# A chunk's final state made in four column groups and brought to its rows by four VectorE instructions

## The chip, the cores and the metric

The kernel runs on one core of a Trainium2 chip, in one launch. The metric is device microseconds of one execution. The engines are named as in the profile: PE (TensorE, matrix products), PEld (its weight loads), DVE (VectorE), ACT (ScalarE), POOL (GpSimd), SP (the queue that issues most DMAs). Three executions of the kernel before took 619.65, 619.74 and 620.53 us; the median is 619.74 us.

## What is computed

The first stage is a state-space scan over 4 batches, 8 heads, 768 tokens, with 32 values of `x` and 16 states for each head. Its output, 3072 rows of 256, goes through two feed-forward layers (256 to 2048 to 256, the first with an ELU, the second with Mish), all in fp32.

```python
for c in range(nc):                      # chunks of tokens
    cum = np.cumsum(la, axis=-1)         # la = log of the clipped decay a
    L = np.exp(cum[:, :, :, None] - cum[:, :, None, :]) * causal
    M = np.einsum('bhin,bhjn->bhij', Cc, Bc) * L
    y_intra = np.einsum('bhij,bhjd->bhid', M, xc)
    y_inter = np.einsum('bhin,bhnd->bhid', Cc, state) * decay_to_i[:, :, :, None]
    y[:, :, sl] = y_intra + y_inter
    Bx = np.einsum('bhjn,bhjd->bhjnd', Bc, xc) * decay_from_j[:, :, :, None, None]
    state = decay_full[:, :, None, None] * state + np.sum(Bx, axis=2)
```

The result doesn't depend on the length of a chunk; the reference uses 32 tokens, the kernel 96.

## The kernel before

**The scan.** A tile `i` is one chunk of 96 tokens of one batch; there are 8 chunks of 4 batches, 32 tiles, and tile `i + 4` is the next chunk of the same batch (`NB` is 4, `T` is 96). Its input `x_t[i]` has 128 rows: rows 0 to 95 are the tokens, 256 columns for the 8 heads; rows 96 to 127 hold the state that came out of the chunk before. A state row belongs to one of the two heads of a pair (16 states each) and has 64 columns for each of the four pairs, in which only the 32 columns of its own head may be other than zero. `rr_t[i]`, as tall, holds the decayed scores of the tokens and, below, the decayed C. So one product over 128 rows (`at_y`, L707) gives a head's within-chunk and from-state parts together. The eight heads' products are 32 rows by 96 columns each; head `h` writes the rows `32 * (h % 4)` on of the PSUM tile `ys`.

**The state.** `at_st` (L737) makes the four pairs' products of `bw_t[i]`, which holds the decayed B of the tokens and, from the second chunk on, the decay of the old state on a diagonal, with `x_t[i]`: 32 rows by 64 columns for a pair. All four are written to rows 96 to 127 of `ys`, side by side in columns 256 to 511. `at_st_out` (L746) is one DVE instruction over 32 rows and 256 columns: it multiplies by the mask `pm`, which keeps each head's own half, and writes rows 96 to 127 of `x_t[i + 4]`. In the last chunk (the last four tiles) no state is made, so there are 28 such tiles. In the first chunk `at_st` of the four tiles stands apart from `at_y`, and the four share one PSUM tile, so each one's products wait for the copy of the one before. From the second chunk on `at_y` and `at_st` are one step on PE, one behind the other, in one buffer of the two of the ring `s`. That buffer is given back when the state's copy and both parts of y (`at_y_hi` on ACT, L719, `at_y_lo` on DVE, L724) have been read; the scores of the next tile (`at_scores0`, L658, in the early tiles; `at_scores`, L670, later) use the same ring, and DVE multiplies them by the decays (L664, L676) before the next `at_y`.

**The feed-forward layers.** They run in blocks of 384, 512 or 256 tokens. A slot is 128 of the 2048 inner columns of a block: `emit_h` (L779 to L781) makes them as three products of split fp32r numbers, ACT and DVE apply the nonlinearity (L795 to L811, L826) and split the outcome (L366, L368, L822), and `emit_y1` (L842 to L847) or `emit_y2` (L873, L874) adds them to the output. The 32 pairs of weight tiles are split on ACT, DVE and POOL as they come in (L340 to L382).

**The order.** No order of instructions is written out: each piece of work is a `step` with an engine (some may choose between two), a planned duration and the steps that it needs; `run_steps` deals them to the engines one after another by these durations and by how late each may begin, and each engine then runs its list in that order. So a step's planned duration doesn't change the work, but it can change the order on every engine. The steps of this change are those at L1099, L1100, L1154 and L1155.

Of the kernel before, what the change touches and what calls it, by code (L numbers as in the profile page):

```python
# [13 lines left out]
ALU = mybir.AluOpType  # L14
# [4 lines left out]
def tile_chain(  # L19
# [12 lines left out]
    nc = tc.nc  # L32
    NB, H, S, D = x.shape
    N = Bm.shape[-1]
    T = 96
# [33 lines left out]
    A, V, G, PE, DQ = "act", "dve", "pool", "pe", "sp"  # L69
# [13 lines left out]
    def step(opts, *deps, dl=1e9):  # L83
        steps.append((opts if isinstance(opts, list) else [opts], deps, dl))
        return len(steps) - 1
# [20 lines left out]
    class Need:  # L106
# [10 lines left out]
        d=Ring(2), r=Ring(1), t=Ring(1), r1=Ring(1), bw=Ring(2), o=Ring(2), stk=Ring(1),  # L117
# [142 lines left out]
    c_t, b_t, c96_t, x_t = {}, {}, {}, {}  # L260
# [468 lines left out]
    def at_st(i):  # L729
        if i == 0:  # L730
            new_ys(i)
        elif i < NB:
            ys_t[i] = ys_t[0]
        kr = 128 if i >= NB else T
        bw, xs = bw_t.pop(i), x_t[i]
        for q in range(H // 2):
            nc.tensor.matmul(  # L737
                out=ys_t[i][T:128, 256 + 64 * q:256 + 64 * q + 64],
                lhsT=bw[0:kr, q, :],
                rhs=xs[0:kr, q * 64:(q + 1) * 64],  # L740
                start=True,
                stop=True,
            )

    def at_st_out(i):
        nc.vector.tensor_tensor(  # L746
            out=x_t[i + NB][T:128].rearrange("p (q e) -> p q e", e=64),
            in0=ys_t[i][T:128, 256:512].rearrange("p (q e) -> p q e", e=64),
            in1=pm[T:128].rearrange("p g d -> p (g d)").unsqueeze(1).to_broadcast([32, H // 2, 64]),
            op=ALU.mult,  # L750
        )


    st = {}
# [199 lines left out]
    for j, (key, k) in enumerate(jobs):  # L954
        rn, pn = [], []
# [141 lines left out]
    for i in range(NB):  # L1097
        bf, bw = BW[i]
        sp_ = step((PE, 0.19, lambda i=i: at_st(i)), bw, LX[i], an, SO.get(i - 1, []))  # L1099
        SO[i] = step((V, 0.41, lambda i=i: at_st_out(i)), sp_, LX[i + NB])  # L1100
        bf.append(sp_)
        xf[i].append(sp_)
    af.append(SO[NB - 1])

    for i in range(NB, tiles):
        c, b = divmod(i, NB)
        bcf, bcn = take("bc")
        lb = step((DQ, 0.96, lambda i=i: load_bc(i), 1.9), bcn)
        l96 = step((DQ, 1.44, lambda i=i: load_c96(i), 0.15), lb)
        d_f, d_n = take("d")  # L1110
        lc = step((DQ, 0.48, lambda i=i: at_cumrow(i), 0.82), s_q4[c], d_n)
        cold = i in TR0
        if cold:
            pf, pn = take("s")
            tr = step((PE, 0.6, lambda i=i: at_tr0(i)), lb, pn)
            tf, tn = take("t")
            a2 = step(alt(lambda e, i=i: at_tr0_out(i, e), (A, 0.37), (V, 0.47)), tr, tn)
            pf.append(a2)
        else:
            a2, a5, tf = three_parts(i, lb)  # L1120
        dd = []
        for g in range(2):
            f = lambda e, i=i, g=g: at_diff(i, g * H // 2, (g + 1) * H // 2, e)
            dd.append(step(alt(f, (G, 1.0), (V, 0.47)), lc, s_q6))
            lock.add(dd[-1])
        mk = step((G, 0.95, lambda i=i: at_mask(i)), dd)
        ex = step((A, 0.78, lambda i=i: at_exp(i)), mk)
        table[ex] = "exp"
        cs = step((G, 0.95, lambda i=i: at_cs(i)), l96, lc, s_d5)
        r_f, r_n = take("r")  # L1130
        rc = step((V, 0.56, lambda i=i: at_rc(i)), cs, r_n)
        rc2 = step(alt(lambda e, i=i: at_rc2(i, e), (V, 0.37), (A, 0.52)), rc)
        lock.add(rc2)
        bcf += [a2, cs]
        if c + 1 < NCH:
            bf, bn = take("bw")
            b1 = step((G, 0.42, lambda i=i: at_bw_1(i)), lb, s_d3, bn)
            b2 = step((G, 0.42, lambda i=i: at_bw_2(i)), s_d7, b1)
            bcf.append(b1)
        if cold:  # L1140
            pz = []
            for z in range(2):
                two = [take("s"), take("s")]
                sc = step((PE, 0.65, lambda i=i, z=z: at_scores0(i, z)), a2, [n for _, n in two])
                tf.append(sc)
                pz.append(step((V, 0.61, lambda i=i, z=z: at_p0(i, z)), sc, ex, r_n))
                for pf, _ in two:
                    pf.append(pz[-1])
        else:
            pz = two_scores(i, a5, tf, ex, r_n, False)  # L1150
        d_f += pz + [rc]
        pf, pn = take("s")
        if c + 1 < NCH:
            y = step((PE, 0.76, lambda i=i: (at_y(i), at_st(i))), pz, rc, rc2, LX[i], pn, SO[i - NB], b1, b2)  # L1154
            SO[i] = step((V, 0.41, lambda i=i: at_st_out(i)), y, LX[i + NB])  # L1155
            pf.append(SO[i])
            bf.append(y)
        else:
            y = step((PE, 0.57, lambda i=i: at_y(i)), pz, rc, rc2, LX[i], pn, SO[i - NB])
        r_f.append(y)  # L1160
        pf += out_of_y(i, y)
        xf[i].append(y)
# [111 lines left out]
```

## Time and profile before

| what | before |
|---|---|
| median of three executions | 619.74 us |
| span of the profiled execution | 618.0 us |
| PE busy | 605.9 us, 98% |
| DVE busy | 433.2 us, 70% |
| ACT busy | 384.6 us, 62% |
| POOL busy | 179.1 us, 29% |
| products of the state, L737 | 224 instructions in 28 tiles |
| copies of the state, L746 | 28 instructions, 430 ns each |

The profile is of one execution whose span, from its first instruction to its last, is 618.0 us, 1.7 us under the median. A line of the profile names the source line, the engine, the operation and what is written from what; `x8` is a number of instructions. A product of fp32 numbers counts as two instructions on PE. Products are pipelined, so the duration of one is longer than the time by which it delays the next; what the chain of waits gives to a group is the time in which it held the path. "Idle before" is how long the engine stood still before an instruction, with what released it.

### The profile page before, as it was taken

How to read it: one execution, taken by the hardware profiler on the slowest of the kernel's cores; microseconds unless marked ns; L12 is line 12 of the kernel's file. 1: busy time of each engine (PE TensorE's matmuls, PEld its weight loads, DVE VectorE, ACT ScalarE, POOL GpSimd, SP SyncE). 2: the span in 40 equal slices, each digit the busy share in tenths (PEclk: the TensorE clock that was granted, in tenths of full speed). 3: DMA queues.
4: the chain of work that ended last, by engine and by line, in shares of the span. 5: the costliest groups of instructions: out<-in, count | busy, mean ns of one | idle time of the engine just before them, and what ended most of it. 6: DMA issues, size and time to landing. Idle time of an engine off the chain costs nothing.

```text
span 618.0 us, 10932 instructions
## 1 busy us (share of the span) xinstructions
PE 605.9 (98%) x3876; PEld 515.0 (83%) x3876; DVE 433.2 (70%) x877; ACT 384.6 (62%) x712; POOL 179.1 (29%) x222
## 2 busy tenths in 40 slices
PE   6999999999999999999999999999999999999997
PEld 5777799899988878888888888888888888988896
DVE  4889899987787788655877865777765445744454
ACT  4699999988788876444596643687544314642121
POOL 2366445332555564011445400236100000200000
PEclk9599999999999999999999999999999999999999
DMA  7699982305467553002474301543300000100010
GB/s 156 175 266 301 295 210 77 60 7 100 104 98 106 104 98 59 2 0 46 77 110 72 82 1 14 108 75 87 60 0 1 1 2 9 27 2 0 1 36 18
DMA packets 133655, 47.09 MB, mean 76 GB/s; under 512 B 116672, under 2 KB 122432, under 8 KB 133600
## 3 DMA queue, kind: packets, MB, share of 16 engines
q1 hardware_dynamic: 133488, 46.29, 34.2%
q8 instruction: 30, 0.49, 0.3%
q14 instruction: 25, 0.20, 0.1%
q10 hardware_dynamic: 112, 0.10, 0.0%
HBM read 32.31 MB, written 3.24 MB: 58 GB/s over the span
## 4 chain that ended last, share of the span: by engine, by line
PE 97%; DMA 1%; DVE 1%; issue 0%; ACT 0%
PE h L779 15%; PE acc L873 15%; PE h L781 14%; PE h L780 14%; PE acc L874 7%; PE acc L842 6%; PE acc L844 6%; PE acc L843 6%; PE acc L847 3%; PE ys L707 3%; PE ys L737 2%; PE s L670 1%; PE s L658 1%; DMA t<-stk 1%; PE p_tr L620 1%; PE p_cr L637 0%
## 5 line engine op out<-in xcount | busy, mean ns | idle before, releaser
L779 PE MATMUL h<-xyh,wi 128*128 128x512 f32 (+2 forms) x448 | 166.9, 373 | 0.0
L780 PE MATMUL h<-xyl,wi 128*128 128x512 f32 (+2 forms) x448 | 161.9, 361 | 0.0
L781 PE MATMUL h<-xyh,wi 128*128 128x512 f32 (+2 forms) x448 | 161.7, 361 | 0.0
L873 PE MATMUL acc<-wo,gh 128*128 128x512 f32 x384 | 142.7, 403 | 0.0
L822 DVE TENSOR_TENSOR gl<-w,gh 128x512 fp32r<-128x512 f32 (+2 forms) x182 | 121.2, 668 | 26.2 <-ACT gh L366 17.2
L826 ACT ACTIVATE w<-h 128x512 f32<-128x512 f32 (+2 forms) x112 | 58.9, 536 | 100.7 <-PE h L781 66.3
L874 PE MATMUL acc<-wo,gl 128*128 128x256 f32 x384 | 107.6, 280 | 0.0
L779 PEld LDWEIGHTS h<-xyh,wi 128*128 128x128 f32 x448 | 84.8, 189 | 14.9 <-DVE g L809 0.2
L368 DVE CAST gh<-w 128x512 fp32r<-128x512 f32 (+2 forms) x110 | 45.3, 412 | 73.8 <-PE acc L873 47.6
L781 PEld LDWEIGHTS h<-xyh,wi 128*128 128x128 f32 x448 | 84.9, 190 | 10.8
L780 PEld LDWEIGHTS h<-xyl,wi 128*128 128x128 f32 x448 | 85.0, 190 | 8.7
L873 PEld LDWEIGHTS acc<-wo,gh 128*128 128x128 f32 x384 | 72.2, 188 | 15.7
L795 ACT ACTIVATE w<-h 128x512 f32<-128x512 f32 (+2 forms) x96 | 51.7, 540 | 47.4 <-PE h L781 33.7
L366 ACT ACTIVATE gh<-w 128x512 fp32r<-128x512 f32 (+2 forms) x98 | 57.4, 586 | 29.3 <-PE acc L843 24.2
L874 PEld LDWEIGHTS acc<-wo,gl 128*128 128x128 f32 x384 | 72.5, 189 | 2.0
L822 POOL TENSOR_TENSOR gl<-w,gh 128x512 fp32r<-128x512 f32 (+2 forms) x26 | 29.7, 1141 | 153.1 <-ACT gh L366 120.2
L842 PE MATMUL acc<-gh,wo 128*128 128x512 f32 (+2 forms) x192 | 70.1, 365 | 0.0
L843 PE MATMUL acc<-gh,wo 128*128 128x512 f32 (+2 forms) x192 | 69.6, 363 | 0.0
L844 PE MATMUL acc<-gl,wo 128*128 128x512 f32 (+2 forms) x192 | 69.6, 362 | 0.0
L803 DVE TENSOR_SCALAR w<-w 128x512 f32<-128x512 f32 (+2 forms) x69 | 28.7, 415 | 26.1 <-ACT w L795 25.2
L811 DVE TENSOR_TENSOR w<-h,w 128x512 f32<-128x512 f32 (+2 forms) x69 | 43.4, 628 | 1.7
L844 PEld LDWEIGHTS acc<-gl,wo 128*128 128x128 f32 x192 | 36.2, 188 | 5.1
(103 smaller groups left out, 847.0 us busy)
## 6 DMA issues: line engine op xcount, KB each, us to landing
d<-cum_d SPq DMA_DIRECT2D x31, 288.0 KB, 3.9
raw<-in_moe_w_in_dram SPq DMA_DIRECT2D x16, 512.0 KB, 6.0
raw<-in_moe_w_out_dram SPq DMA_DIRECT2D x16, 512.0 KB, 6.1
xs<-in_x_dram SPq DMA_DIRECT2D x32, 96.0 KB, 2.9
bc<-in_C_dram SPq DMA_DIRECT2D x32, 48.0 KB, 3.1
bc<-in_B_dram SPq DMA_DIRECT2D x32, 48.0 KB, 3.0
out_dram<-o SPq DMA_DIRECT2D x15, 96.0 KB, 1.9
bc<-bc SPq DMA_DIRECT2D x84, 16.0 KB, 2.3
```

The lines of the kernel that those rows point to most:

```text
L366: nc.scalar.activation(out=out, in_=in_, func=AF.Copy)
L779: nc.tensor.matmul(out=h, lhsT=hi[:, k, fs], rhs=xh[:, k, :], start=(k == 0), stop=False)
L780: nc.tensor.matmul(out=h, lhsT=hi[:, k, fs], rhs=xl[:, k, :], start=False, stop=False)
L781: nc.tensor.matmul(out=h, lhsT=lo[:, k, fs], rhs=xh[:, k, :], start=False, stop=(k == 1))
L795: nc.scalar.activation(out=new_w(s), in_=st[s][0], func=AF.Exp)
L822: alu(eng).tensor_tensor(out=gl, in0=w, in1=gh.bitcast(F32), op=ALU.subtract)
L826: nc.scalar.activation(out=new_w(s), in_=st[s][0], func=AF.Mish)
L842: nc.tensor.matmul(out=y, lhsT=hi[:, f % FP, ds], rhs=gh, start=(f == 0), stop=False)
L843: nc.tensor.matmul(out=y, lhsT=lo[:, f % FP, ds], rhs=gh, start=False, stop=False)
L844: nc.tensor.matmul(out=y, lhsT=hi[:, f % FP, ds], rhs=gl, start=False, stop=(f == NF - 1))
L873: nc.tensor.matmul(out=y, lhsT=gh[:, ts], rhs=w[:, :, f % FP, :], start=(f == 0), stop=False)
L874: nc.tensor.matmul(out=y[:, 0], lhsT=gl[:, ts], rhs=w[:, 0, f % FP, :], start=False, stop=(f == NF - 1))
```

## The change

Pair `q` of the state is written to rows `32 * q` to `32 * q + 31` of `ys`, in columns 256 to 319, so each of the four products has a column group of its own. As the four pairs no longer stand on one set of rows, the copy into rows 96 to 127 of the next chunk's tile becomes four DVE instructions of 32 rows and 64 columns, each from another set of rows. The planned durations follow: the copy's from 0.41 to 0.95 us, that of `at_y` with `at_st` from 0.76 to 0.65 us.

```diff
     def at_st(i):
...
         for q in range(H // 2):
             nc.tensor.matmul(
-                out=ys_t[i][T:128, 256 + 64 * q:256 + 64 * q + 64],
+                out=ys_t[i][32 * q:32 * q + 32, 256:320],
                 lhsT=bw[0:kr, q, :],
                 rhs=xs[0:kr, q * 64:(q + 1) * 64],
...
     def at_st_out(i):
-        nc.vector.tensor_tensor(
-            out=x_t[i + NB][T:128].rearrange("p (q e) -> p q e", e=64),
-            in0=ys_t[i][T:128, 256:512].rearrange("p (q e) -> p q e", e=64),
-            in1=pm[T:128].rearrange("p g d -> p (g d)").unsqueeze(1).to_broadcast([32, H // 2, 64]),
-            op=ALU.mult,
-        )
+        for q in range(H // 2):
+            nc.vector.tensor_tensor(
+                out=x_t[i + NB][T:128, 64 * q:64 * q + 64],
+                in0=ys_t[i][32 * q:32 * q + 32, 256:320],
+                in1=pm[T:128].rearrange("p g d -> p (g d)"),
+                op=ALU.mult,
+            )
...
-        SO[i] = step((V, 0.41, lambda i=i: at_st_out(i)), sp_, LX[i + NB])
+        SO[i] = step((V, 0.95, lambda i=i: at_st_out(i)), sp_, LX[i + NB])
...
-            y = step((PE, 0.76, lambda i=i: (at_y(i), at_st(i))), pz, rc, rc2, LX[i], pn, SO[i - NB], b1, b2)
-            SO[i] = step((V, 0.41, lambda i=i: at_st_out(i)), y, LX[i + NB])
+            y = step((PE, 0.65, lambda i=i: (at_y(i), at_st(i))), pz, rc, rc2, LX[i], pn, SO[i - NB], b1, b2)
+            SO[i] = step((V, 0.95, lambda i=i: at_st_out(i)), y, LX[i + NB])
```

## Rows read from the trace of the kernel before

**Rows 1.** The page: busy us, share of the span and instructions of each engine.

```profile
PE 605.9 (98%) x3876; PEld 515.0 (83%) x3876; DVE 433.2 (70%) x877; ACT 384.6 (62%) x712; POOL 179.1 (29%) x222
```

**Rows 2.** Waits of PE: line and what it waited for, us in total, times, longest.

```profile
PE p_cr L637 <- DVE cum L439: 4.4, 1, 4.4
...
PE s L658 <- DVE r L664: 0.9, 1, 0.9
...
PE ys L707 <- DVE r L676: 0.4, 1, 0.4
PE p_d L493 <- ACT dk L366: 0.2, 1, 0.2
```

**Rows 3.** The chain that ended last, whole span: shares by line.

```profile
by line: PE h L779 15.1%; PE acc L873 14.9%; PE h L781 14.3%; PE h L780 14.3%; PE acc L874 7.2%; PE acc L842 6.3%; PE acc L844 6.2%; PE acc L843 6.2%; PE acc L847 3.3%; PE ys L707 2.6%; PE ys L737 2.1%; PE s L670 1.5%; PE s L658 1.5%; DMA t
```

**Rows 4.** The chain from 154 to 161 us: start, us, what.

```profile
155.43 0.47 PE ys L707 x16
155.90 0.45 PE ys L737 x8
156.34 0.38 PE h L779
...
159.67 0.36 PE s L670 x8
```

**Rows 5.** L707 in short stretches: stretch, length, busy us (instructions in flight) of PE.

```profile
155.34:155.40 0.06, 0.04 (x4) 0.04 (x7) 1.00 1.09 307
...
155.62:155.66 0.04, 0.04 (x16) 0.04 (x4) 1.00 0.16 39
```

**Rows 6.** The same view of L737, two of its first stretches.

```profile
155.72:155.78 0.06, 0.05 (x1) 0.06 (x2) 1.00 0.37 111
...
155.89:155.95 0.06, 0.06 (x4) 0.06 (x3) 1.00 0.95 248
```

**Rows 7.** The same view of L658, four products on two row groups.

```profile
64.01:64.10 0.09, 0.08 (x2) 0.08 (x2) 1.00 0.54 147
...
64.18:64.20 0.02, 0.02 (x4) 0.02 (x5) 1.00 1.63 419
```

**Rows 8.** The chain from 22 to 37 us: the first chunk's state products.

```profile
23.57 0.99 PE ys L737 x8
...
35.18 0.90 PE ys L737 x16
```

**Rows 9.** L746 by stretch: stretch, length, busy us (instructions) of DVE.

```profile
0.00:137.00 137.00, 3.87 (x9) 0.95 0.65 175
```

**Rows 10.** All engines by stretch: PE, PEld, DVE, ACT, POOL busy us, granted clock.

```profile
24.00:137.00 113.00, 112.50 (x730) 97.21 (x728) 102.87 (x203) 105.69 (x201) 55.92 (x58) 0.98 0.63 173
137.00:420.00 283.00, 282.33 (x1836) 236.26 (x1835) 206.47 (x405) 190.08 (x338) 100.81 (x129) 1.00 0.39 71
```

**Rows 11.** Groups on DVE by shape: out and in, number, busy us, mean ns, idle before.

```profile
L746 DVE TENSOR_TENSOR xs<-ys,pm 32x256 f32<-32x256 f32 x28 | 12.1, 430 | 11.3 <-ACT xyh L719 5.9 <-PE ys L737 4.9
L724 DVE SCALAR_TENSOR_TENSOR xyl<-ys,xyh 128x192 fp32r<-128x192 f32 x29 | 10.3, 354 | 1.4 <-ACT xyh L719 1.0
L724 DVE SCALAR_TENSOR_TENSOR xyl<-ys,xyh 128x64 fp32r<-128x64 f32 x3 | 0.7, 221 | 1.0 <-ACT xyh L719 1.0
```

**Rows 12.** DVE in order of time: start, us, instruction.

```profile
22.08 0.68 DVE L382 TENSOR_TENSOR wi<-raw,wi 128x512 fp32r<-128x512 f32 x1
22.68 0.35 DVE L724 SCALAR_TENSOR_TENSOR xyl<-ys,xyh 128x192 fp32r<-128x192 f32 x1
...
33.95 0.43 DVE L746 TENSOR_TENSOR xs<-ys,pm 32x256 f32<-32x256 f32 x1
34.41 0.70 DVE L358 SCALAR_TENSOR_TENSOR raw<-raw 128x512 int32<-128x512 int32 x1
...
157.35 0.36 DVE L724 SCALAR_TENSOR_TENSOR xyl<-ys,xyh 128x192 fp32r<-128x192 f32 x1
```

**Rows 13.** The stretch of the low granted clock: engines as in rows 10.

```profile
15.25:28.90 13.65, 12.66 (x127) 10.32 (x124) 11.71 (x31) 8.72 (x19) 3.94 (x4) 0.50 0.61 162
```

## The prediction

> **What bounds the kernel now.** I read the page's busy shares and slices first [rows 1]. PE is busy in 605.9 of 618.0 us; DVE has 70% and ACT 62%. The span is 1.7 us short of the median of the runs shown (619.74); what lies around the span I take as constant, so a gain in the span is a gain in the median. Then PE's waits: six in all, from 4.4 us to 0.2, together 7.6 us, of which the 4.4 us is the start; the other five make 3.2 us [rows 2]. So for nearly the whole span nothing else makes PE wait, and a microsecond of PE work taken away is a microsecond off the span, until another engine becomes late. The chain that ended last says the same: PE's lines fill it, and L737, the line that the change touches, has 2.1% of it, 13.0 us [rows 3]. Last I read engines by stretch [rows 10], because DVE and ACT don't have the same room everywhere. Until 137 us the weights are prepared and PE, ACT and DVE are all near full (112.5, 105.7 and 102.9 of 113 us from 24 us on); from 137 to 420 us PE is full and DVE has 206.5 of 283.
>
> **The removed PE time.** In an ordinary tile the chain holds the 16 instructions of L707 (eight heads, two instructions each) for 0.47 us and then the 8 of L737 (four pairs, two each) for 0.45 us [rows 4]. Twice the instructions, half as wide again, in the same time: the counts of instructions in flight show why. L707's enter four at a time: 4 are begun in the first 0.06 us and 16 after 0.3 [rows 5]. Its heads go to column groups 0, 1, 2, 3 in turn. L737's enter one at a time, 1 in the first 0.06 us and 4 after 0.2 [rows 6]; all four pairs go to column group 3, so each waits for the one in front. The change gives pair q column group q. It should then go as L707 does, in two rounds of four. That this also holds for four products only, both instructions of each, is seen at L658: four products on two row groups enter in pairs, 2 and then 4 [rows 7]. It isn't the same arrangement, but it shows that the second instruction of a product doesn't stand between its neighbours' first ones.
>
> A round should take what one instruction takes now, 0.45 / 8 = 0.056 us; two rounds 0.11 us, and 0.34 us is saved in a tile. The bounds for two rounds: 0.11 us, and two of L707's rounds at full width, 2 x 0.47 / 4 = 0.24 us, which holds also the change from the wide product in front. I take 0.11, because L737 mostly follows L707 directly, and the change to the next wide product (0.38 us, [rows 4]) is paid now as then. The first tile ran at half the granted clock [rows 13]: 0.99 us [rows 8], and six instructions fewer of twice 0.056 us save 0.67 there. Sum: 0.67 + 27 x 0.34 = 9.9 us of the 13.0. Of the 28 tiles [rows 11] 9 lie before 137 us [rows 9] and 19 behind: 0.67 + 8 x 0.34 = 3.4 us early, 19 x 0.34 = 6.5 us late.
>
> **The added DVE time.** One instruction of 32x256 took 430 ns. What four of 32x64 take no row shows. Above, each could cost the whole 430; below, a quarter of it, and then nothing is added (less is excluded, since the same elements are read). L724 reads the same tile at several widths: 354 ns at 192 and 221 at 64 [rows 11], which is 1.04 ns an element, and L746's 430 at 256 lies on the same line. So I take 0.22 us each. Do they overlap? Many neighbours on DVE do: an instruction of 0.68 us from 22.08 was followed at 22.68. After L746 it isn't so: 0.43 us from 33.95, the next at 34.41 [rows 12]. I take the second kind, 0.25 us from start to start, so 1.0 us for four against 0.46 now: 0.54 us more in each tile, 15 us in all. The Trainium skill gives this a rule ("VectorE: DVE Perf Modes", section "Two Vector instructions with no wait between them"): an instruction that starts in another quadrant (a set of 32 rows) of a memory than the one before it is held until all earlier ones are done. The gap after L746, which writes rows 96 to 127, agrees; the four new ones each read another quadrant, so by the rule they would not overlap either.
>
> Where the 0.54 us lie: behind 137 us DVE has 76 us of idle time for 19 x 0.54 = 10.3, and nothing on PE waits for L746 directly, as its rows are read four tiles later. The PSUM buffer of a tile is held 0.54 us longer: in the tile above L724, the last to read it, ended at 157.71 [rows 12], and the next scores came at 159.67 [rows 4], so 1.4 of 2.0 us remain. In the first four tiles, which share one buffer, the next product waits for the copy: the copy from 33.95 ended at 34.38 and the chain reached the next L737 at 35.18 [rows 8, 12], so some 0.3 of 0.8 us remain. I cost both at nothing; without that cover each tile would pay up to 0.54. Behind the four instructions on DVE stand the lower half of the split of y (L724), the products of scores and decays (L676) and the FFN's elementwise steps, and PE waits for those.
>
> Before 137 us it is different. DVE would have 102.9 + 9 x 0.54 = 107.8 us of work in 113 - 3.4 = 109.6: 98%. ACT would stand at 105.7 of 109.6, 96%. That is room on paper only; it is where the next engine is late. Bounds for the early part: all of 3.4 us gained, or none of it and 4.9 us of DVE added to the path. DVE's idle 10.1 us there is more than what is added, so I stay nearer the first end and take half, 1.7 us.
>
> **The planner.** Step costs change (0.41 to 0.95 for the copy, 0.76 to 0.65 for the products), so the order on all engines is dealt anew. The trace can't show the new order. Its price is bounded by PE's waits inside the span: the 3.2 us may vanish, or come twice. I take zero.
>
> **The forecast.** 6.5 + 1.7 = 8.2 us: span 609.8, median 619.74 - 8.2 = 611.5.
>
> **The rivals.**
> - DVE becomes the bound until 137 us. For it: 98% on paper, ACT beside it. Against: PE waited for DVE only 0.9 + 0.4 us there and later [rows 2], and the planner may move steps to POOL (55.9 of 113 us). None of the early gain and up to 4.9 us lost: 613.2 to 618.1, middle 615.7. The Trainium skill warns of this turn ("TensorEngine Tiling (Array Packing)", section "PSUM Bottleneck"): tiling speeds up TensorE but not the emptying of PSUM. No row shows that it binds here.
> - The change doesn't do what it says: only the second instruction of one pair runs beside the first of the next, so five rounds stand in place of two and half of the saving goes: 4.9 us less, or 4.1 after the same discount early, 615.6. For it: a product's two instructions need the same column group. Against: rows 5 and 7. The skill's "TensorE: Matmul & The Clock Gate" (Part 3) says that products start strictly in program order; if a pair's two instructions stood next to each other there, this case would follow, and L707's rounds of four speak against it.
> - Slower: the 0.54 us stand in front of DVE work that PE waits for in every tile. The place is the scores' product (L664, L676) before L707; PE has waited for it, 0.9 and 0.4 us, twice [rows 2]. If every tile paid all of it, 28 x (0.54 - 0.34) = 5.6 us are lost: 625.3. It decides where the added wait of a tile passes 0.34 us. Against: two waits in 32 tiles.
> - More than counted: PE's present waits vanish as well, 9.9 + 3.2 us: 606.6.
> - The clock: PE is granted half speed (0.50, that is 1.2 of 2.4 GHz) from 15.25 to 28.9 us [rows 13], after the thin work of the start. The first product group lies in it and gets shorter. If the low stretch became half as long again, some 7 us of work would cost 3.4 us more, and as long again 6.8: 618.3 at worst.
>
> **How the numbers follow.** Chances: forecast 0.60 (608.3 to 614.7: all of the early part to none, and 1.5 us of planner either way), DVE bound 0.15, pairs only 0.07, slower 0.09, more than counted 0.05, clock 0.04. The range of 8 in 10 takes the forecast, nearly all of the second and the third case: 607.5 to 617.5. About 0.2%, 1.24 us, is what a measurement of this kernel can tell from no change, so "faster" means below 618.5: 0.60 + 0.14 + 0.06 + 0.05 + 0.01 = 0.86; within 0.05; slower 0.09.
>
> **What would show it.** L737's 8 instructions on the chain at 0.11 to 0.15 us instead of 0.45, in two rounds of four, and its share of the span at some 3 us; five rounds and 0.28 us would be the pairs. L746 with 112 instructions near 220 ns, 0.25 us apart; 430 each would bring 36 us onto DVE. PE still with few waits after 137 us. Between 24 and 137 us: whether the stretch that prepares the weights ends earlier by 3.4 us, or PE shows waits for DVE or ACT there. The forecast is wrong if PE waits at L707 or at the scores in tile after tile, or if the granted clock at the start stays low past 29 us.

## The result and the profile after

The changed kernel takes 624.46 us (median of five runs, 623.10 to 626.97) beside 619.83 us of the kernel before (619.65 to 622.05). The ratio is 1.0067, with an interval of 1.0052 to 1.0082: some 4.5 us slower, where 8.2 us less were forecast. The profiled execution took 624.2 us, its span is 622.5. Behind L746 the source lines stand one further down: the copy is L747, the products of `emit_h` are L780 to L782, those of `emit_y1` L843 to L845, those of `emit_y2` L874 and L875.

The page of after, engines and chain of waits (for the engines, [rows 1]; for the shares of the chain, [rows 3]):

```profile
PE 602.3 (97%) x3876; PEld 508.4 (82%) x3876; DVE 450.5 (72%) x948; ACT 377.3 (61%) x705; POOL 191.6 (31%) x238
...
PE 77%; DVE 6%; ACT 6%; DMA 4%; issue 3%; SPq 2%; POOL 1%; DVEq 0%; POOLq 0%; ACTq 0%
```

Before, PE's lines filled the chain. Now they hold 77% of it, and the rest leads through DVE, ACT, DMAs and their issue. The time in which PE was not busy (span less busy) was 618.0 - 605.9 = 12.1 us; it is 622.5 - 602.3 = 20.2. So PE has 3.6 us less to do and stands still 8.1 us longer, which makes the 4.5.

PE's waits in after (columns as in [rows 2]; the first is the start):

```profile
PE p_cr L637 <- DVE cum L439: 4.3, 1, 4.3
PE acc L843 <- DVE xyl L859: 3.0, 1, 3.0
...
PE s L658 <- DVE r L664: 1.3, 3, 0.9
PE s L670 <- DMA t<-stk: 1.2, 2, 0.7
...
PE s L670 <- DVE xyl L724: 0.8, 1, 0.8
...
PE ys L737 <- DVE xs L747: 0.4, 1, 0.4
...
PE ys L707 <- DVE r L664: 0.3, 1, 0.3
```

Behind the start there were 3.2 us of waits; all the rows of this view now make 10.7. Most of the new ones are for DVE: for the output of a block, which must be read before its PSUM is written again (L859), the lower half of the split of y (L724), the products of scores and decays (L664), the copy itself (L747). No place repeats in every tile.

The change itself did what it was meant to do. The chain of after in one tile, for [rows 4], and the groups of L737 and of the copy:

```profile
161.21 0.47 PE ys L707 x16
161.67 0.11 PE ys L737 x8
161.78 0.37 PE h L780
```

```profile
L737 PE MATMUL ys<-xs,bw 128*32 128x64 f32 x192 | 7.2, 219 | 0.0
L747 DVE TENSOR_TENSOR xs<-ys,pm 32x64 f32<-32x64 f32 x112 | 25.0, 223 | 14.2 <-PE ys L737 7.4 <-ACT xyh L719 5.2
```

The eight instructions hold the path for 0.11 us in place of 0.45. The four copies are 223 ns each and do not overlap, as DVE in order of time shows, for [rows 12]:

```profile
161.85 0.94 DVE L747 TENSOR_TENSOR xs<-ys,pm 32x64 f32<-32x64 f32 x4 [0.37 <-PE ys L737]
```

0.94 us for four, against 0.43 for the one before: some 0.5 us more in a tile, 28 x 0.5 = 14 us in all. (0.54 was forecast.)

### The profile page after: what moved, and what is told of

Read it like the earlier page. It is cut to its first block, busy times and chain, and to the rows that moved or that the text cites. A ratio compares the mean times of both kernels' runs of the same rounds, so it can differ in the third digit from the quotient of the medians.

```text
span 622.5 us, 10990 instructions
## 1 busy us (share of the span) xinstructions
PE 602.3 (97%) x3876; PEld 508.4 (82%) x3876; DVE 450.5 (72%) x948; ACT 377.3 (61%) x705; POOL 191.6 (31%) x238
## 4 chain that ended last, share of the span: by engine, by line
PE 77%; DVE 6%; ACT 6%; DMA 4%; issue 3%; SPq 2%; POOL 1%; DVEq 0%; POOLq 0%; ACTq 0%
PE acc L874 13%; PE h L780 12%; PE h L781 12%; PE h L782 12%; PE acc L875 6%; PE acc L843 6%; PE acc L844 6%; PE acc L845 6%; PE ys L707 2%; DMA t<-stk 1%; DMA bc<-in_B_dram 1%; PE s L670 1%; DMA xs<-in_x_dram 1%; DVE gl L823 1%; DVE raw L358 1%
## 5 line engine op out<-in xcount | busy, mean ns | idle before, releaser
L780 PE MATMUL h<-xyh,wi 128*128 128x512 f32 (+2 forms) x448 | 168.6, 376 | 2.0 <-ACT w L827 1.6
L782 PE MATMUL h<-xyh,wi 128*128 128x512 f32 (+2 forms) x448 | 161.7, 361 | 0.0
L874 PE MATMUL acc<-wo,gh 128*128 128x512 f32 x384 | 142.6, 403 | 0.0
L823 DVE TENSOR_TENSOR gl<-w,gh 128x512 fp32r<-128x512 f32 (+2 forms) x181 | 119.2, 660 | 20.9 <-ACT gh L366 13.0
L827 ACT ACTIVATE w<-h 128x512 f32<-128x512 f32 (+2 forms) x112 | 59.4, 536 | 103.0 <-PE h L782 67.8
L875 PE MATMUL acc<-wo,gl 128*128 128x256 f32 x384 | 107.7, 280 | 0.2 <-DVE gl L823 0.2
L368 DVE CAST gh<-w 128x512 fp32r<-128x512 f32 (+2 forms) x114 | 47.8, 420 | 74.6 <-PE acc L874 50.3
L780 PEld LDWEIGHTS h<-xyh,wi 128*128 128x128 f32 x448 | 84.8, 189 | 19.0 <-ACT w L827 3.6
L782 PEld LDWEIGHTS h<-xyh,wi 128*128 128x128 f32 x448 | 84.9, 189 | 10.6
L874 PEld LDWEIGHTS acc<-wo,gh 128*128 128x128 f32 x384 | 72.2, 188 | 15.4
L823 POOL TENSOR_TENSOR gl<-w,gh 128x512 fp32r<-128x512 f32 (+2 forms) x27 | 31.2, 1156 | 173.3 <-ACT gh L366 112.2
L875 PEld LDWEIGHTS acc<-wo,gl 128*128 128x128 f32 x384 | 72.6, 189 | 2.7 <-DVE gl L823 0.5
L843 PE MATMUL acc<-gh,wo 128*128 128x512 f32 (+2 forms) x192 | 71.0, 370 | 3.0 <-DVE xyl L859 3.0
L366 ACT ACTIVATE gh<-w 128x512 fp32r<-128x512 f32 (+2 forms) x94 | 54.8, 583 | 28.8 <-PE acc L844 22.5
L845 PE MATMUL acc<-gl,wo 128*128 128x512 f32 (+2 forms) x192 | 70.2, 366 | 0.0
L844 PE MATMUL acc<-gh,wo 128*128 128x512 f32 (+2 forms) x192 | 70.2, 365 | 0.0
L804 DVE TENSOR_SCALAR w<-w 128x512 f32<-128x512 f32 (+2 forms) x74 | 32.9, 444 | 26.0 <-ACT w L796 25.0
L812 DVE TENSOR_TENSOR w<-h,w 128x512 f32<-128x512 f32 (+2 forms) x74 | 46.6, 631 | 1.5
L843 PEld LDWEIGHTS acc<-gh,wo 128*128 128x128 f32 x192 | 36.7, 191 | 8.4 <-DVE xyl L859 3.4
```

What stands on the lines that cost most here:

```text
L366: nc.scalar.activation(out=out, in_=in_, func=AF.Copy)
L780: nc.tensor.matmul(out=h, lhsT=hi[:, k, fs], rhs=xh[:, k, :], start=(k == 0), stop=False)
L782: nc.tensor.matmul(out=h, lhsT=lo[:, k, fs], rhs=xh[:, k, :], start=False, stop=(k == 1))
L823: alu(eng).tensor_tensor(out=gl, in0=w, in1=gh.bitcast(F32), op=ALU.subtract)
L827: nc.scalar.activation(out=new_w(s), in_=st[s][0], func=AF.Mish)
L843: nc.tensor.matmul(out=y, lhsT=hi[:, f % FP, ds], rhs=gh, start=(f == 0), stop=False)
```

## The experiments

Two theories stood at first. D: the copies' DVE time is on the path. R: the new order, dealt from the new durations, is to blame, and in the old order the change gains. All ratios are to the kernel before in the same session, whose median was 620.9 to 621.4 us.

### The order: e1, e2, e4

e1 has the change's work with the old durations, so every engine runs in the order of before. e2 has the old work with the new durations, so the order of after.

```diff
# e1, against after
-        SO[i] = step((V, 0.95, ...
+        SO[i] = step((V, 0.41, ...
-            y = step((PE, 0.65, ...
+            y = step((PE, 0.76, ...
# e2, against before: the same two durations the other way round
# e4, against after: only the copy's 0.95 becomes 0.41
```

> The change's work (four column groups, four copies) with the planned durations of before (0.41, 0.76), so that every engine runs its list in the order of before. Theory R (the newly dealt order lost the gain): PE keeps most of the 9.9 us that the products save, 610 to 613 us, and the 3.0 us wait of L843 for L859 and the low clock near 89 us are gone. Theory D (0.5 us more of DVE in each tile is what makes DVE late until 137 us, whatever the order): 617 to 624 us, with PE waiting for DVE between 60 and 130 us.

> The work of before (one column group, one copy) with the planned durations of the change (0.95, 0.65), so the order of the changed kernel. R: slower than before, 623 to 631 us: the waits of the new order stand, and 9.9 us of PE are not saved, of which the idle time takes up a part. D: within 1.5 us of before, 619 to 621 us, since DVE has its old load.

> The changed kernel with only the copy's planned duration put back to 0.41 (products stay at 0.65): a third order, of the same work. R: a time of its own, anywhere from 609 to 622 us, with other waits at other places. D: within 1.5 us of the changed kernel, 623 to 626 us.

| kernel | median us | ratio |
|---|---|---|
| e1, change in the order of before | 626.57 | 1.0077 (1.0050 to 1.0105) |
| e2, old work in the order of after | 624.42 | 1.0049 (1.0034 to 1.0064) |
| e4, change in a third order | 623.30 | 1.0033 (1.0022 to 1.0044) |

R falls with e1: in the old order the change loses as much as in the new. (It is slower even than the 617 to 624 us that D gave it.) D alone doesn't do either, as it has no place for what e2 shows: with the new order 3.0 us are lost with no change in the work. Its longest new wait stands where after has its longest:

```profile
PE acc L842 <- DVE xyl L858: 1.5, 1, 1.5
```

Not all of e2's 3.0 us are waits: its four executions had a mean granted clock of 0.984 to 0.986, the seventeen of before in the same session 0.987 to 0.991. In its profile the low stretch at the start is 3.4 us longer, worth some 1.7 us (last section).

So the change loses in three orders, by 2 to 5 us; the order decides at which waits.

### The two halves of the change: e3, e5, e15

All in the order of before. e3 makes the four copies from one column group. e5 makes the four column groups but keeps one copy of 32x256; it reads the last pair's block four times, so the states of the other three pairs are left out of its computation. e15 is e5 with that one copy made twice.

```diff
# e3, against before
-        nc.vector.tensor_tensor(
-            out=x_t[i + NB][T:128].rearrange("p (q e) -> p q e", e=64),
...
+        for q in range(H // 2):
+            nc.vector.tensor_tensor(
+                out=x_t[i + NB][T:128, 64 * q:64 * q + 64],
+                in0=ys_t[i][T:128, 256 + 64 * q:256 + 64 * q + 64],
...
# e5, against before
-                out=ys_t[i][T:128, 256 + 64 * q:256 + 64 * q + 64],
+                out=ys_t[i][32 * q:32 * q + 32, 256:320],
...
-            in0=ys_t[i][T:128, 256:512].rearrange("p (q e) -> p q e", e=64),
+            in0=ys_t[i][T:128, 256:320].unsqueeze(1).to_broadcast([32, H // 2, 64]),
# e15, against e5
+        for _ in range(2):
             nc.vector.tensor_tensor(
```

> Before with one part of the change: four copies of 32x64 in place of one of 32x256, products still in one column group, order of before. R: 619 to 621 us, DVE takes the 14 us in its idle time. D: 622 to 626 us. Each copy should last about 220 ns either way.

> Order of before; the products in four column groups, but one copy of 32x256 as before, which takes the last pair's block four times (so the state is wrong: three pairs' copies are left out, the instructions and their sizes are those of before). PE saves 9.9 us and DVE has its old load. Theory A (the copies' DVE time is what eats the gain): 8 to 10 us faster than before, ratio 0.984 to 0.988. Theory B (the lists are dealt so that DVE and the DMAs come just in time for a PE that is slower than planned; a faster PE only waits for them): less than 4 us faster, ratio 0.993 to 1.003, with more PE waits than before.

> As the run with the groups alone (order of before, four column groups, a copy of 32x256 that takes the last pair's block four times, so three pairs' copies are left out), with that one copy made twice: 0.46 us more of DVE in each tile, as four copies of 32x64 bring, but no copy from another set of rows and two instructions instead of four. If it is DVE's time: as slow as the change in this order, 623 to 628 us, against 615.1 with one copy. If it is the sets of rows or the number of instructions: 615 to 619 us.

| order of before | one copy | four copies (last row: two of 32x256) |
|---|---|---|
| one column group | before, 621.1 to 621.4 | e3 622.59, ratio 1.0019 (1.0009 to 1.0028) |
| four column groups | e5 615.11, ratio 0.9902 (0.9887 to 0.9917) | e1 626.57, ratio 1.0077 (1.0050 to 1.0105) |
| four groups, one copy twice | | e15 629.62, ratio 1.0144 (1.0124 to 1.0163) |

This is the study's main table. Once the products are fast the four copies cost 5.1 + 6.0 = 11.2 us. e15 adds nearly the same DVE time in another form (24.0 us in place of some 12, row below) and loses at least as much, 14.5 us against e5, more than was expected of it. So with fast products it is DVE's added time that costs, whether it comes as four instructions from four sets of rows or as two from one set.

```profile
L747 DVE TENSOR_TENSOR xs<-ys,pm 32x256 f32<-32x256 f32 x56 | 24.0, 429 | 7.2 <-ACT xyh L719 3.4 <-PE ys L737 2.2
```

With slow products the four copies cost 1.2 us (e3), but that is not the price of the same DVE time. In e3 all four read one set of rows, and they overlap: 112 of 223 ns each take 18.6 us together, 0.66 us a tile; in e1 and after, where each reads another set, they take 25.0 us, 0.94 a tile.

```profile
L747 DVE TENSOR_TENSOR xs<-ys,pm 32x64 f32<-32x64 f32 x112 | 18.6, 223 | 8.5 <-ACT xyh L719 4.3 <-PE ys L737 3.5
```

So e3 adds 6.5 us to DVE and loses 1.2, e1 adds 13.0 to e5 and loses 11.2. The loss for each added us is far larger with fast products (0.9 against 0.2), but no run adds 13 us beside slow ones: how much of the difference is the faster PE's and how much the larger addition's stays open. e5's 6.0 us is also less than theory A's 8 to 10 and more than theory B's 4: with no DVE time added PE still has new waits.

PE's waits in e5 and in e1, the longest rows of each:

```profile
PE s L670 <- DVE xyl L724: 1.5, 2, 1.0
...
PE acc L842 <- DVE xyl L858: 0.6, 1, 0.6
```

```profile
PE ys L707 <- DVE r L676: 2.4, 2, 2.0
PE s L670 <- DVE xyl L724: 2.4, 3, 1.3
PE acc L843 <- DVE xyl L859: 2.2, 1, 2.2
PE s L670 <- DMA t<-stk: 1.9, 1, 1.9
```

The same places stand in e15, with nearly the same waits (2.3 us for L724, 2.2 for L859, 1.8 for the DMA, 1.7 for L676). A ledger of the profiled executions, in us (that of e15 was the shortest of its four, 627.27 us, that of e1 nearly the longest, 627.95):

| | span | PE busy | PE not busy | DVE: copies | DVE: all else | stretches at 0.50 behind a wait |
|---|---|---|---|---|---|---|
| before | 618.0 | 605.9 | 12.1 | 12.1 | 421.1 | none |
| e3 | 621.0 | 606.2 | 14.8 | 18.6 | 419.7 | none |
| e5 | 613.4 | 598.5 | 14.9 | 12.0 | 421.7 | none |
| e1 | 626.2 | 602.8 | 23.4 | 25.0 | 425.7 | two of 3.4 us |
| e15 | 625.5 | 603.0 | 22.5 | 24.0 | 424.7 | two |
| after | 622.5 | 602.3 | 20.2 | 25.0 | 425.5 | one |

From e5 to e1: 8.5 us more standing still (all rows of the two views of waits, without the start, make 14.3 and 5.8), and 4.3 us more busy, of which two stretches at half the granted clock account for 2 x 1.7 = 3.4. That is 11.9 of the 12.8 us between the spans. The clock alone is not the loss: one execution of e1 had the mean granted clock of before, 0.989 (e5's four had 0.988), and took 625.02 us, still 9.9 more than e5.

Why average idle time was no cover is seen in one window of e1, for [rows 10], same columns:

```profile
137.00:420.00 283.00, 275.47 (x1803) 228.65 (x1802) 214.20 (x449) 185.04 (x330) 103.49 (x132) 0.99 0.38 68
```

From 137 to 420 us DVE is idle for 283 - 214.2 = 68.8 us, and PE stands still for 7.5 us all the same (0.7 before). The idle time lies where DVE has nothing to do; the waits lie where DVE runs without a pause towards a step that PE needs next.

Of what such a wait is made can be read too, as DVE does the same work in the same order in before and e1. DVE in order of time from a tile's copy to the step that L842 (in e1 L843) needs, first before, then e1:

```profile
76.06 0.43 DVE L746 TENSOR_TENSOR xs<-ys,pm 32x256 f32<-32x256 f32 x1
...
80.40 0.68 DVE L358 SCALAR_TENSOR_TENSOR raw<-raw 128x512 int32<-128x512 int32 x1
...
82.68 1.01 DVE L858 SCALAR_TENSOR_TENSOR xyl<-acc,xyh 128x384 fp32r<-128x384 f32 x2
```

```profile
76.79 0.93 DVE L747 TENSOR_TENSOR xs<-ys,pm 32x64 f32<-32x64 f32 x4
...
82.17 1.53 DVE L358 SCALAR_TENSOR_TENSOR raw<-raw 128x512 int32<-128x512 int32 x1
...
85.78 1.01 DVE L859 SCALAR_TENSOR_TENSOR xyl<-acc,xyh 128x384 fp32r<-128x384 f32 x2
```

DVE runs without a pause in both. This work lasts 7.63 us before and 10.00 in e1, 2.4 more. The copies of the one tile in it are 0.5 of that; the other 1.9 are the same instructions taking longer. At e1's wait for L676 near 235 us it is 2.1 us more (3.83 and 5.96 from the copy to the end of L676), again 0.5 of it copies. So the copies start the loss, as e5 and e1 differ in nothing else, but where PE waits longest most of the delay is DVE's other instructions, run at another moment and for longer (last section).

### Early and late tiles: e6, e7

The change in the first nine tiles only (e6), or in the other nineteen only (e7), order of before.

```diff
# e6, against e1 (e7: i >= 9)
-                out=ys_t[i][32 * q:32 * q + 32, 256:320],
+                out=ys_t[i][32 * q:32 * q + 32, 256:320] if i < 9 else ys_t[i][T:128, 256 + 64 * q:256 + 64 * q + 64],
```

> Order of before; the change (four groups, four copies) only in the 9 tiles until 137 us, the other 19 as before. If DVE as the bound until 137 us is the whole loss: as slow as the full change in this order, 3 to 6 us slower than before (ratio 1.005 to 1.010). If the loss is spread over all tiles: within 2.5 us of before.

> Order of before; the change only in the 19 tiles after 137 us. The forecast's step (DVE has 76 us of idle time there, so all of 6.5 us is gained) says 5 to 7 us faster, ratio 0.989 to 0.992. Theory B says no gain: PE's waits in front of the scores and of L707 take it, ratio 0.998 to 1.006.

e6: 623.98 us, ratio 1.0049 (1.0035 to 1.0063), 2.8 us lost. e7: 625.24 us, 1.0057 (1.0037 to 1.0078), 4.1 us lost. Each part loses on its own, the late one too, which was to bring 6.5 us (which of them loses more their intervals don't tell). e6 lies between its two cases, e7 in the range of theory B. Their longest waits, e6 and then e7:

```profile
PE acc L851 <- DVE xyl L867: 2.2, 1, 2.2
```

```profile
PE ys L707 <- DVE r L676: 2.7, 2, 2.3
PE s L670 <- DVE xyl L724: 2.5, 3, 1.3
```

Together these are e1's list: the early tiles cause the wait for the block's output (L867 here is L859 of e1), the late ones those for L676 and L724.

### Half of it: e10, e16

Two column groups and two copies of 32x128. e16 is the same with durations to match (0.62 and 0.70).

```diff
# e10, against before
-        for q in range(H // 2):
+        for q in (0, 2, 1, 3):
-                out=ys_t[i][T:128, 256 + 64 * q:256 + 64 * q + 64],
+                out=ys_t[i][64 + 32 * (q // 2):96 + 32 * (q // 2), 256 + 64 * (q % 2):320 + 64 * (q % 2)],
```

> Order of before; two column groups, two copies of 32x128 instead of four of 32x64. PE saves half of the rounds (0.22 us a tile, 6.3 us in all), DVE gets about 0.15 us more in each tile (two of some 0.29 us, 0.03 us between them). If the cost goes with DVE's added time as between one and four copies at four groups (11.5 us for 28 times 0.5): 6.1/9.9 of 6.3 gained, 3.4 lost: 0 to 1.5 us faster than before, ratio 0.996 to 1.001. If it needs four copies to fall into waits: 3 to 5 us faster.

> The two column groups with planned durations near what they take (0.62 for the copies, 0.70 for the products): another order of the same work, for a version better than both. If a dealing with true durations is better: 612 to 618 us. If each dealing has stalls of its own, a few us either way of the 619.8 of the order of before: 616 to 626 us.

e10: 619.77 us against 621.09, ratio 0.9980 (0.9966 to 0.9994), 1.3 us gained. e16: 621.14, ratio 1.0007 (0.9995 to 1.0019). Its groups show the trade:

```profile
L747 DVE TENSOR_TENSOR xs<-ys,pm 32x128 f32<-32x128 f32 x56 | 16.5, 294 | 7.4 <-ACT xyh L719 4.5 <-PE ys L737 2.0
L737 PE MATMUL ys<-xs,bw 128*32 128x64 f32 x192 | 9.4, 219 | 0.0
```

Before, L737's line was this:

```profile
L737 PE MATMUL ys<-xs,bw 128*32 128x64 f32 x192 | 14.6, 219 | 0.0
```

Two thirds of PE's gain (14.6 to 9.4 us, where four groups reach 7.2) for a third of DVE's price (12.1 to 16.5, where four copies reach 25.0). It is the fastest kernel of the study that computes everything, and by little: e10's five executions at a mean granted clock of 0.989 to 0.992 took 618.0 to 619.7 us, its five at 0.984 to 0.986 took 619.9 to 621.5, and before's thirteen, at 0.987 to 0.990, 620.1 to 621.9. In the profiled one, of the faster five, the low stretch at the start is 10.2 us long in place of 13.65, worth more than the 1.3 us. The order of e16 takes the gain away again.

### Taking the work off DVE: e8, e9, e11, e12, e13

e8 keeps the four groups, masks all 128 rows in one DVE instruction and lets four small DMAs bring the blocks to their rows; e9 is that in an order dealt with 0.25 and 0.65. e11 to e13 do the mask in the products (B padded with zeros for the other head, eight products in place of four), so that plain copies are left: e11 gives two of the four to ACT, in all tiles; e12 the same in the late nineteen tiles only; e13 gives all four to ACT, late tiles only (the masked products stand in all tiles of all three).

```diff
# e8, against before, beside the four column groups
+        g = at.tile([128, 64], F32, tag="stg", name="stg", bufs=2)
         nc.vector.tensor_tensor(
+            out=g, in0=ys_t[i][:, 256:320], in1=pm.rearrange("p g d -> p (g d)"), op=ALU.mult
+        for q in range(H // 2):
+            nc.sync.dma_start(out=x_t[i + NB][T:128, 64 * q:64 * q + 64], in_=g[32 * q:32 * q + 32])
# e11 and e12 (e13: A for all four)
+        for q in range(H // 2):
+            copy(V if q % 2 else A, x_t[i + NB][T:128, 64 * q:64 * q + 64], ys_t[i][32 * q:32 * q + 32, 256:320])
```

> Four column groups, order of before, and DVE lighter than before: one instruction over all 128 rows and 64 columns (L724 at 64 columns took 221 ns) masks the state into a tile of its own, and four small DMAs on SP bring its sets of 32 rows to the rows 96 to 127 of the next chunk. If DVE's time is what eats the gain, this keeps at least the gain of the groups alone: 609 to 615 us, ratio 0.981 to 0.991. If the transfers come late or SP's queue stands behind DVE: 616 to 625 us, with PE waits for DMAs that before does not have.

> The same work as the run with the light copy and DMAs, with planned durations near what the two steps now take (0.25 for the copy, 0.65 for the products): a newly dealt order. If the order matters little once DVE has room: within 3 us of that run. If each dealing has its own stalls: 5 us or more apart.

> Order of before; four column groups in all tiles; the mask is made in the product (each head's 16 columns of the decayed B beside 16 of zeros, eight products of 32 columns in place of four of 64), so that the copies are plain, two on DVE and two on ACT. DVE has about its load of before (two of some 0.22 us against 0.43), ACT gets some 0.4 us a tile more. If DVE's time alone eats the gain: near the groups alone, 3 to 7 us faster than before (ratio 0.989 to 0.995). If any engine that is late will do, ACT (105.7 of 113 us until 137 us) takes it: 0 to 5 us slower.

> As the run with half of the copies on ACT, but only in the 19 tiles after 137 us; the early tiles keep one column group and one copy on DVE. The late tiles of the groups alone brought some 2.7 us. If DVE's time decides: 2 to 5 us faster than before. If it is the number of instructions behind y's product, on whatever engine: 0 to 4 us slower, as the change in the late tiles was (4.1 us slower).

> As the run before, with all four copies of the 19 late tiles on ACT, so that DVE has 0.46 us a tile less than before. If DVE's time decides: the most of all, 4 to 7 us faster than before (ratio 0.989 to 0.994). If ACT's list in turn holds up the exponentials: less than with half on ACT, or slower.

| kernel | median us | ratio |
|---|---|---|
| e8 | 656.01 | 1.0569 (1.0538 to 1.0601) |
| e9 | 643.17 | 1.0353 (1.0315 to 1.0392) |
| e11 | 636.34 | 1.0260 (1.0211 to 1.0310) |
| e12 | 628.56 | 1.0125 (1.0096 to 1.0153) |
| e13 | 622.65 | 1.0031 (1.0015 to 1.0046) |

Of e8 and e11 to e13 none came near the gain expected for the case that DVE's time decides, and e8, e11 and e12 are slower than either of their cases. e9 is 12.8 us faster than e8, by its order alone.

In e8 DVE's part is light, 28 instructions of 217 ns. But the DMAs stand in SP's queue, and the queue stands still in front of them until DVE is done (22.5 us in the two rows below); what is queued behind comes late. PE's waits make 33 us behind the start, of which the largest row, 8.8 us, is for a DMA; most of the rest are for DVE and ACT, and how many of these go back to late transfers wasn't traced. Its group on DVE, and from the view of waits those of SP at the new DMAs (L753) and PE's longest, for a DMA:

```profile
L749 DVE TENSOR_TENSOR stg<-ys,pm 128x64 f32<-128x64 f32 x28 | 6.1, 217 | 4.4 <-PE ys L739 2.2 <-ACT xyh L721 2.2
```

```profile
SPq L753 <- DVE xyl L726: 12.2, 7, 3.1
SPq L753 <- DVE stg L749: 10.3, 5, 2.9
```

```profile
PE s L672 <- DMA t<-stk: 8.8, 5, 3.7
```

e11 and e12 are confounded. Dealing the copies of one tile to two engines made them wait for each other; DVE's group of e12:

```profile
L368 DVE COPY xs<-ys 32x64 f32<-32x64 f32 x38 | 8.6, 225 | 22.7 <-ACT xs L366 22.5
```

DVE stood still for 22.5 us in front of 38 copies, waiting for ACT's copy into the same tile. So these two say nothing on whether ACT has room. e13 has no such alternation: 622.65 against e7's 625.24, the same tiles with the copies on DVE. Moving the time away from DVE may bring some of it back (the intervals, 1.0015 to 1.0046 and 1.0037 to 1.0078, overlap), but not a gain; e13 also has 224 more instructions on PE, and ACT has its own steps that PE waits for (L833 below is L827 of e1):

```profile
PE h L786 <- ACT w L833: 2.4, 4, 1.1
PE ys L713 <- DVE r L682: 2.3, 2, 1.9
```

The Trainium skill says in "TensorEngine Tiling (Array Packing)", section "PSUM Bottleneck", that after such a gain the copying out of PSUM may become the bottleneck, and that both ScalarE and VectorE should do it. The first half holds here, by e5 against e1 (11.2 us); the second as tried in e11 and e12 made the kernel slower, and e13, with all copies of the late tiles on ACT, was no gain either.

## Why the prediction was wrong, step by step

**The bound: right for the kernel before, and no further.** PE was the bound [rows 1 to 3]. The inference that a microsecond of PE work is a microsecond off the span "until another engine becomes late" had that point at a distance; it was right there. e5, with no DVE time added, takes 7.4 us off PE's busy time and 4.6 off the span: 2.8 us come back as waits. The margin was less than the saving.

**The removed PE time: right in the tile.** 0.45 to 0.11 us, the price of two rounds of four; "pairs only" falls with it. The sum was 9.9 us; PE's busy time fell by 7.4 in e5. Where the other 2.5 are the runs don't tell: a busy PE counts instructions in flight, not time on the path.

**The added DVE time: right.** 0.22 us each was forecast, 223 ns measured; no overlap, 0.94 us for four. That each reads another set of rows mattered, as the prediction had it: from one set, in e3, four took 0.66.

**What hides it: the step that failed.** The late part was taken as gained in full, 6.5 us, because DVE has 76 us of idle time for 10.3. e7 is that part alone: 4.1 us lost, 10.6 us from the forecast. Two things were wrong in the step. An idle share of a 283 us window was used as cover for additions at 19 fixed places, and idle time elsewhere covers nothing. And the margin of the scores' buffer was read from one tile (1.4 of 2.0 us left, [rows 4, 12]) and taken for all: that tile's is not the smallest, and in e7 PE waits for L724 three times, up to 1.3 us. The price without the cover stood in the text ("each tile would pay up to 0.54", 15 us in all), and it wasn't given weight; e1 against e5 shows 11.2. The sum also had no term for DVE's other instructions, which took longer in front of the waits: of the 2.4 and 2.1 us by which DVE was later at e1's two places above, 1.9 and 1.6 are theirs. The cover was priced against the kernel before, though the change makes PE faster. That PE's slow products were what DVE hid behind fits e3's small loss, but isn't shown, as e3 adds only half of the time.

**The early part: wrong.** Half of 3.4 us was to be gained. e6 loses 2.8; its profile shows one long wait (2.2 us for L867), one of 1.2 for L818, and the low clock behind the first. The low clock isn't needed for the loss: two of its six executions had a mean granted clock of 0.992, above all of before's, and took 623.03 and 623.44 us. "98%, room on paper only" was read rightly, and then set at half.

**The planner: its value wrong, its bound held by luck.** Zero, within 3.2 us either way; e2 costs 3.0. But these are not the old waits come twice: e2 has one new wait of 1.5 us and a longer low stretch at the start. With the change's work the orders of e1, after and e4 lie at ratios 1.0077, 1.0067 and 1.0033.

**The rivals.** "Slower" named the right engine and nearly the right time (625.3; 624.46 was measured), but not the place: it wanted 0.2 us in every tile at the scores' product before L707. In after PE waits there for L664 a single time, 0.3 us. What decides is not an added wait of 0.34 us in a tile but a few places without margin, where a wait of 1 to 3 us stands at once; at e1's two, most of the delay is DVE's other instructions, not the copies. That the total came out near is chance. "DVE becomes the bound until 137 us" had the mechanism and a stretch that was too short: it goes on behind 137 us, as e7 shows. "The clock" had the right price and the wrong place: the stretch at the start was as long in after, about 1 us later (a mean of 0.54 in the window of [rows 13]), and new ones came behind PE's waits. So the clock stayed low past 29 us, a sign that the prediction named, without costing more there.

**The sum.** Without the copies' cost the forecast of 8.2 us is not far from e5's 6.0. With them it is 12.8 us off, of which the copies beside fast products are 11.2 in the order of before.

## What to carry to other kernels

When a change takes time off the bounding engine and puts time on another, price the other engine's addition against the kernel as it will be, with the bound already faster: do the two halves alone and together, and see that each half adds what it adds in the whole (here the copies alone took 6.5 us of DVE, in the whole 13.0): a loss of 1.2 us and a gain of 6.0 made a loss of 5.1. Read the second engine's margin at every place where the first one needs its outcome, and take the smallest; the idle share of a window doesn't give it. Between the ends there may be a better trade (two groups, two copies: 1.3 us gained).

## What the runs showed of the hardware that was not expected

**The granted clock fell behind a single wait of PE.** In after, windows around the longest wait; columns as in [rows 10]:

```profile
84.90:88.40 3.50, 0.45 (x4) 0.13 (x2) 3.50 (x4) 1.70 (x4) 2.38 (x3) 0.95 0.93 154
88.40:92.40 4.00, 4.00 (x15) 4.00 (x16) 3.40 (x7) 2.61 (x5) 0.00 (x0) 0.61 1.05 210
```

PE stands still for 3.05 us, and from 88.1 us, shortly before it works on, it gets half the clock (1.2 in place of 2.4 GHz) for 3.4 us; its products come every 0.32 us in place of 0.17. That costs another 1.6 us. e1 has two such falls, behind waits of 2.24 and 1.86 us; the second:

```profile
179.90:182.60 2.70, 0.84 (x11) 0.51 (x10) 1.73 (x4) 1.40 (x4) 1.80 (x2) 1.00 1.00 163
182.60:186.00 3.40, 3.40 (x13) 3.11 (x12) 2.28 (x7) 2.30 (x6) 0.89 (x2) 0.50 0.13 23
```

But the wait of 2.04 us for L676, at 235 us in e1, was not followed by one:

```profile
234.95:237.40 2.45, 0.41 (x4) 0.01 (x2) 2.45 (x4) 0.60 (x1) 1.56 (x2) 1.00 0.09 20
237.40:240.80 3.40, 3.31 (x35) 2.53 (x36) 3.37 (x10) 1.33 (x3) 1.38 (x2) 1.00 0.52 123
```

So a long wait can cost nearly twice itself, and by these rows its length alone doesn't decide it.

**The low stretch at the start is not of one length.** It ended at 28.9 us before [rows 13]. In e3 it ended earlier, in e2 later, as one window of each shows, columns as above:

```profile
25.45:28.90 3.45, 3.45 (x24) 3.11 (x25) 3.32 (x10) 1.70 (x5) 1.87 (x2) 0.80 0.31 54
```

```profile
28.90:32.30 3.40, 3.40 (x17) 2.79 (x17) 0.98 (x2) 2.43 (x5) 2.52 (x4) 0.56 0.89 209
```

A stretch of 3.4 us at half the clock is worth 1.7 us, so some 1.7 of e2's 3.0 us can be the clock's and not the waits'. Each execution's mean granted clock is on record, though not its stretches: e2's four have 0.984 to 0.986, so all of them had more low clock than before's (0.987 to 0.991); e3's ten have 0.987 to 0.992, and the four at 0.990 and more took 621.9 to 622.7 us, the six others 621.8 to 623.5, so its cost hangs little on it. Why the length differs stays open; e1, e5 and e15 have the stretch of before within a few tenths of a us, after has it about 1 us later, and the main comparison, e5 with e1, doesn't hang on it.

**DVE's instructions stretch.** In front of that wait in after, DVE ran from 81.98 us without a pause, and some of its instructions took far longer than elsewhere; POOL worked beside it:

```profile
77.17 0.93 DVE L747 TENSOR_TENSOR xs<-ys,pm 32x64 f32<-32x64 f32 x4
...
81.98 0.80 DVE L804 TENSOR_SCALAR w<-w 128x384 f32<-128x384 f32 x1 [0.16 <-ACT w L796]
82.70 1.54 DVE L368 CAST wi<-raw 128x512 fp32r<-128x512 f32 x1
...
84.64 1.50 DVE L823 TENSOR_TENSOR gl<-w,gh 128x384 fp32r<-128x384 f32 x1
86.06 1.78 DVE L382 TENSOR_TENSOR wi<-raw,wi 128x512 fp32r<-128x512 f32 x1
87.76 1.01 DVE L859 SCALAR_TENSOR_TENSOR xyl<-acc,xyh 128x384 fp32r<-128x384 f32 x2
```

L382 on the same shape took 0.68 us at 22.08 in the kernel before [rows 12], 1.78 here. The copies aren't in this run of work: behind those of 77.17 DVE stood still again, the last time for 0.16 us before 81.98. So the longest wait of after isn't copies that queue up in front of it, and e2, with the old copies in this order, waits at the same place (1.5 us). The stretching is not new either, and it goes with POOL: in before and in after alike ten of DVE's L382 on this shape had no POOL work beside them and took 0.67 to 0.69 us; the eight and nine others took from 0.68 up to 1.32 and 1.78. L811 (L812 in after), on 128x384, which reads one operand from PSUM, stayed at 0.54 to 0.56 with and without POOL. What the copies do is to move DVE's work to other moments. That POOL is the cause is still only argued: no run took POOL's work away.
